# Six PSUM banks of an attention kernel: two each for scores, maxima and the rest, against three by ScalarE and three by VectorE

## The chip, the core and the metric

The kernel runs on one core of a Trainium2 chip. TensorE (PE) multiplies matrices and writes its results into PSUM, which has eight banks here, each holding a tile of 128 partitions x 512 fp32 numbers. ScalarE (ACT) and VectorE (DVE) empty the banks; GpSimd (POOL) works on on-chip memory alone, and SyncE (SP) issues most transfers. The metric is the time of one execution on the device, in microseconds (us). In the profile, PEld is the loading of a weight operand, which runs beside PE.

## What is computed

Attention in which a query sees only the keys of its own hash bucket, then a mixture of eight experts with one expert for each token. Cut to what matters:

```
q_bits = einsum('bhsd,dk->bhsk', q, proj) > 0          # B, H, S, D = 4, 8, 768, 64; 6 bits
k_bits = einsum('bhsd,dk->bhsk', k, proj) > 0
mask   = bucket(q_bits)[..., :, None] == bucket(k_bits)[..., None, :]
scores = where(mask, q @ k.T / sqrt(D), -1e9)
attn   = exp(scores - max); attn = attn / (attn.sum(-1) + 1e-9)
x      = (attn @ v) as 3072 tokens x 512
logits = x @ w_gate + modality_bias[modality_id]; e = argmax(logits); g = softmax(logits)[e]
out    = g * (relu(x @ w1[e]) @ w2[e])                  # 8 experts, 512 -> 1024 -> 512
```

## The kernel before

**Staging.** The 32 heads are worked on as 16 pairs (about 28 us each), then the experts follow. While pair i is scored, the maxima of pair i+1 are taken and pair i+2 is prepared; the weighing of pair i by V lags a few steps. Every four pairs a batch element is finished (`finish`, `finish_x`, `route`).

**The tiles in PSUM.** For each pair there are
- 18 tiles of scores (`score`, L280 and L281, tile `pss`), each emptied by one exponential on ScalarE (L292 or L299). A third of them ("rest") hold 256 columns of both heads;
- 4 pattern products (`patterns`, L207, tile `psx`): the hash bits, multiplied by a pattern, are written beside q and k by two ScalarE operations each (L208, L209);
- 18 tiles of maxima (`maxp`, L224 and L230, tile `psm`), each emptied by one reduction on VectorE (L226 or L232);
- 2 broadcasts of the maxima (`maxp_back`, L249, tile `psx`; "first" with 512 columns and "second" with 256), read by three VectorE operations each (L251 twice, L252);
- one tile each for the bits (L187), the sums of V (L267) and the row sums (L344), in `psx`;
- and what finishing a batch element needs (L359, L367, L385, L403, L598), in `psx`.

Two more banks (`psu`) accumulate the weighing (L326) throughout.

**The banks.** `ps_s` holds two banks for `pss`, `ps_m` two for `psm`, `ps_x` two for everything called `psx`. A pool hands out its banks in turn: a tile takes the bank of the tile two places before it in the same pool, and its first matmul waits until the readers of that older tile are done.

**What sets the order.** PE and SP execute in the order in which the code is written: the strings of `PLAN` (one for each of the six key tiles of a pair) say which generator takes its next step, S a score tile, M a maximum, T or P a step of preparation, B a broadcast, A a step of weighing, V the sums of V, Q the row sums. The last string of a pair ends with `SMTSMTSMBAAB`, the first of the next begins with `LvSPM`: the second and third pattern, the first broadcast, two steps of weighing, the second broadcast, and then the last pattern. ACT, DVE and POOL each execute in an order of their own, which is set when the program is built, from the same code.

**Other lines named later.** L161 copies q or k to a rounded high part `hx` on ScalarE, L163 subtracts it to get the low part (768 columns, both inputs in on-chip memory; on POOL or DVE, and in pairs 9, 10, 13 and 14 on DVE for both halves), L242 spreads the maxima for the broadcast, L302 adds the exponentials into row sums (mostly on POOL, two operations for a key tile).

Of the kernel before, what the change touches and what calls it, by code (L numbers as in the profile page):

```python
# [9 lines left out]
F32 = mybir.dt.float32  # L10
# [6 lines left out]
PSUM = bass.MemoryType.PSUM  # L17

B, H, S, D = 4, 8, 768, 64
NT = S // 128  # L20
HALF = S // 2
MAIN = 512
REST = S - MAIN
NP = B * H // 2
BIG = 2.0 ** 100
CFG = dict(spd=(15,), fxs=3, wy=(0.3, 0.71), hpf=0, he=0, hn=0, hm=0, avp=(1, 2, 3, 4, 5, 6), avs=(2,), early=2, pj=7, w3=(0, 0.9), x3=(0, 1), nmd=1, man=(), man0=2, hpo=0, hpe=0, p0=(0, 1), p1=(0, 0.25), p2=(0, 0.4), p3=(0.4, 0.9), s0=4, rc='DDDD', rq=(1, 2), tq=(3, 3, 1, 1, 0, 0), wh=(0.5, 0.78), ws=(0.78, 1.05), n2=2, psx=2, psm=2, pss=2, npb=5, ut=8, qk=3, v=3, wm=(0, 0.9), wf=(0.04, 1.02), wx=(0.3, 0.71), sub="DPPD", fx='D', fx3='R', raw=4, wp=7, LS=4, LL=7, pn=0, rv=(0,), rs='DDPP', r1=(0, 0.5), r2=(0, 1), avg=1, fub=2, fd=1, pm=(), fj=0, fxe=0.5)
P = 128
# [48 lines left out]


def attention(ctx, actx, tc, a, x_d, route, setup, early_slots, early_tables, latest, adds, bias):
    nc = tc.nc
    v = a["v"]  # L80
# [16 lines left out]
    const = actx.enter_context(tc.tile_pool(name="const", bufs=1))  # L97
    ps_m = actx.enter_context(tc.tile_pool(name="ps_m", bufs=CFG["psm"], space=PSUM))
    ps_s = actx.enter_context(tc.tile_pool(name="ps_s", bufs=CFG["pss"], space=PSUM))
    flags = actx.enter_context(tc.tile_pool(name="flags", bufs=2))  # L100
# [81 lines left out]
    def signs(i):  # L182

        t = st[i]
        z = ps_x.tile([P, MAIN], F32, name="psx")
        for o in range(4):
            nc.tensor.matmul(z[32 * o:32 * o + 32, 0:HALF], zst, t["x"][:, o // 2, (o % 2) * HALF:(o % 2 + 1) * HALF],  # L187
                             start=True, stop=True, tile_position=(0, 32 * o))
        nc.vector.tensor_scalar(out=bits[i % 2], in0=z[:, 0:HALF], scalar1=0.0, scalar2=0.5, op0=ALU.is_gt, op1=ALU.subtract)
        yield  # L190
# [9 lines left out]
    def patterns(i):  # L200

        t = st[i]
        for half in range(2):
            hs = slice(half * HALF, (half + 1) * HALF)
            for h in range(2):
                pp = ps_x.tile([P, MAIN], F32, name="psx")
                nc.tensor.matmul(pp[:, 0:HALF], pat[:, half, h], bits[i % 2], start=True, stop=True)  # L207
                (nc.vector.tensor_copy if i == 0 else nc.scalar.copy)(out=t["m1"][h][PT[h], hs], in_=pp[0:64, 0:HALF])  # L208
                nc.scalar.activation(t["s1"][h][PT[h], hs], pp[64:128, 0:HALF], AF.Relu)  # L209
                if half == 0 and h == 1:  # L210
                    move(t["b"][0][QK[1], 0], t["a"][0][QK[0], 0])
                    move(t["b"][1][QK[0], 1], t["a"][1][QK[1], 1])
                yield

    def maxp(i, late):
# [4 lines left out]
        for qt in range(0, NT, 2):  # L220
            for h in range(2):
                for j in range(2):
                    mp = ps_m.tile([P, MAIN], F32, name="psm")
                    nc.tensor.matmul(mp, t["m1"][h][:, (qt + j) * P:(qt + j + 1) * P], t["s1"][h][:, 0:MAIN], start=True, stop=True)  # L224
                    with tc.high_priority(offset=CFG["hm"]):
                        newest[:] = [nc.vector.tensor_reduce(out=mx[:, qt + j, 1 - h, 0:1], in_=mp, axis=AX.X, op=ALU.max).ins]  # L226
                    yield
                mp = ps_m.tile([P, 2, REST], F32, name="psm")
                for j in range(2):
# [16 lines left out]
    def maxp_back(t, nm, n, cs):  # L246
        bc = ps_x.tile([P, MAIN], F32, name="psx")
        for j in range(n):
# [14 lines left out]
    def vsums(i):  # L263

        a2, vs = st[i]["va"], vsb[i % 2]
        vp = ps_x.tile([P, MAIN], F32, name="psx")
        nc.tensor.matmul(vp[:, 0:P], ones32, a2.rearrange("p h d -> p (h d)"), start=True, stop=True)  # L267
# [69 lines left out]
    def sums(i):  # L337

        b, c = i // 4, i % 4
        if c == 0:  # L340
            gsum[b] = bp.tile([P, HALF], F32, name="gs")
        g = ps_x.tile([P, MAIN], F32, name="psx")
        for j in range(4):
# [7 lines left out]
    def finish(b):  # L351
# [3 lines left out]
        for part in range(2):  # L355
            hs = (slice(0, MAIN), slice(MAIN, S))[part]
            g = ps_x.tile([P, MAIN], F32, name="psx")
            for c in range(4):
# [5 lines left out]
        rv = rin.rearrange("p (a j) (c h) -> p a j c h", a=2, h=2)  # L364
        tp = ps_x.tile([P, 4, P], F32, name="psx")
        for j in range(3):
# [12 lines left out]
        for w in range(2):  # L379
            n = 4 if w == 0 else 2  # L380
            ts = slice(4 * w, 4 * w + n)
            tp = ps_x.tile([P, 4, P], F32, name="psx")
            for j in range(n):
# [6 lines left out]
        yield  # L390
        yield from route(b, lg, ps_x)

    def finish_x(b, lo, hi, pool=bp, n=2, name="xs"):
# [3 lines left out]
        for tt in range(lo, hi):  # L397
            if done:
                done.pop()()
            xs = pool.tile([P, 512], F32, name=name, bufs=n)  # L400
            xp = ps_x.tile([P, 512], F32, name="psx")
            for c in range(4):
# [31 lines left out]
    with tc.manual_schedule(engines={mybir.EngineType.PE, mybir.EngineType.SP}):  # L434
# [17 lines left out]
        avs = weigh()  # L452
# [44 lines left out]
        for _ in avs:  # L497
            pass
        sums(NPR - 1)
    return finish, finish_x, ps_x, ident  # L500


# [518 lines left out]
```

## Time and profile before

| | |
|---|---|
| Median of 3 runs | 800.71 us (800.22 to 800.9) |
| The profiled execution | 798.11 us, of which 796.3 us are its span |
| Granted clock of TensorE over the span | 0.994 |
| Busy share of the span | PE 94%, PEld 66%, DVE 63%, POOL 55%, ACT 52% |

In the page PE reads 9 in nearly every one of the 40 slices. That is not PE at its peak: a matmul of 512 columns is drawn with 0.39 to 0.50 us, but the next one starts 0.23 us after it, so that waits shorter than the overlap disappear from the idle time. Waits are read from the distance of starts.

### The profile page before, as it was taken

To read this page: it belongs to the slowest core of one execution; us is meant where nothing else is said; L and a number is where in the kernel's file an instruction comes from. 1 tells how busy PE (TensorE), PEld (TensorE's weight loads), DVE (VectorE), ACT (ScalarE), POOL (GpSimd) and SP (SyncE) were. 2 spreads that over 40 slices of the span, in tenths; PEclk is the share of its full clock that TensorE was granted. 3 is DMA by queue.
4 is the path that set the end of the run, shared out by engine and by line. 5 is a ranking of instruction groups with operands and counts; after the bars stand their busy time and mean duration, and the time that the engine had idled before them with its cause. 6 is when DMAs were issued, how large, how long until landed. Compare 5 with 4: busy or idle time off the path is not lost.

```text
span 796.3 us, 11626 instructions
## 1 busy us (share of the span) xinstructions
PE 748.0 (94%) x4060; PEld 522.6 (66%) x4060; DVE 505.0 (63%) x839; ACT 413.6 (52%) x730; POOL 438.9 (55%) x321
## 2 busy tenths in 40 slices
PE   4799999999999999997899899999999999999996
PEld 1555556566655566654555555888888888888885
DVE  5777677587787769778769859764244342752422
ACT  3566666666557566664446455324253334633323
POOL 7198988788779978697857694034220204202002
PEclk9999999999999999999999999999999999999999
DMA  6665544254347524465310276466443535833321
GB/s 204 154 179 159 159 119 129 71 159 113 103 123 160 136 83 117 126 153 121 93 48 14 63 161 218 155 90 229 132 159 86 165 101 173 278 134 123 130 54 60
DMA packets 59572, 104.24 MB, mean 131 GB/s; under 512 B 9709, under 2 KB 30829, under 8 KB 59504
## 3 DMA queue, kind: packets, MB, share of 16 engines
q1 hardware_dynamic: 53424, 88.23, 40.0%
q0 software_dynamic: 4928, 13.14, 5.1%
q10 hardware_dynamic: 1152, 2.03, 0.9%
q8 instruction: 34, 0.56, 0.3%
q14 instruction: 34, 0.28, 0.1%
HBM read 59.89 MB, written 13.33 MB: 92 GB/s over the span
## 4 chain that ended last, share of the span: by engine, by line
PE 68%; DVE 11%; issue 10%; ACT 6%; DMA 2%; SPq 1%; POOL 1%; POOLq 0%; ACTq 0%; DVEq 0%
PE psu L326 12%; PE pss L280 8%; PE pss L281 6%; PE hps L812 5%; PE hps L813 5%; PE hps L811 5%; PE yps L857 4%; PE yps L855 4%; PE yps L856 4%; PE psm L224 4%; ACT pb L292 3%; PE psm L230 2%; DVE mx L226 1%; DVE a_0g L251 1%; PE psx L344 1%
## 5 line engine op out<-in xcount | busy, mean ns | idle before, releaser
L302 POOL TENSOR_TENSOR sp<-sp,pb 128x768 f32<-128x768 f32 x124 | 230.9, 1887 | 35.6 <-ACT pb L299 32.2
L292 ACT ACTIVATE pb<-pss 128x512 f32<-128x512 f32 x192 | 113.8, 598 | 104.8 <-PE pss L281 89.4
L226 DVE TENSOR_REDUCE mx<-psm 128x1 f32<-128x512 f32 x192 | 130.7, 687 | 55.2 <-PE psm L224 54.2
L764 DVE TENSOR_TENSOR w<-raw,w 128x1024 fp32r<-128x1024 f32 x64 | 79.5, 1249 | 94.9 <-ACT w L762 66.5
L326 PE MATMUL psu<-pb,vt 128*64 128x512 f32 (+1 forms) x768 | 134.4, 492 | 0.0
L762 ACT CAST w<-raw 128x1024 fp32r<-128x1024 f32 x64 | 66.9, 1050 | 73.8 <-PE yps L857 62.4
L326 PEld LDWEIGHTS psu<-pb,vt 128*64 128x64 f32 x768 | 50.8, 136 | 69.1 <-issue 58.8
L782 POOL DMA_INDIRECT xg<-x_d,tb x18 | 21.9, 1219 | 117.7 <-DMA tb<-tab 113.4
L280 PE MATMUL pss<-a_0g 128*128 128x512 f32 x192 | 80.4, 419 | 3.5 <-ACT pb L292 2.2
L855 PE MATMUL yps<-w,hl 128*128 128x512 f32 x208 | 82.7, 398 | 0.0
L302 POOL TENSOR_TENSOR sp<-pb,pb 128x768 f32<-128x768 f32 x31 | 58.9, 1918 | 41.0 <-ACT pb L299 40.9
L857 PE MATMUL yps<-w,hh 128*128 128x512 f32 x208 | 81.3, 391 | 0.0
L856 PE MATMUL yps<-w,hh 128*128 128x512 f32 x208 | 81.0, 389 | 0.0
L812 PE MATMUL hps<-xl,w 128*128 128x512 f32 x192 | 74.8, 390 | 1.4 <-DVE xl L801 1.4
L811 PE MATMUL hps<-xh,w 128*128 128x512 f32 x192 | 75.5, 393 | 0.0
L813 PE MATMUL hps<-xh,w 128*128 128x512 f32 x192 | 74.8, 390 | 0.0
L232 DVE TENSOR_REDUCE mx<-psm 128x2 f32<-128x512 f32 x96 | 66.1, 689 | 9.6 <-PE psm L230 7.4
L280 PE MATMUL pss<-a_1g 128*128 128x512 f32 x192 | 68.3, 356 | 3.7 <-ACT pb L299 3.4
L817 ACT ACTIVATE hh<-hps 128x512 fp32r<-128x512 f32 x48 | 28.7, 598 | 74.0 <-PE hps L813 71.8
L281 PE MATMUL pss<-b_0g 128*128 128x512 f32 x192 | 65.9, 343 | 0.0
L281 PE MATMUL pss<-b_1g 128*128 128x512 f32 x192 | 65.7, 342 | 0.0
L818 DVE SCALAR_TENSOR_TENSOR hl<-hps,hh 128x512 fp32r<-128x512 f32 x48 | 33.0, 688 | 51.1 <-ACT hh L817 50.5
(203 smaller groups left out, 1374.3 us busy)
## 6 DMA issues: line engine op xcount, KB each, us to landing
raw<-moe_w SPq DMA_DIRECT2D x64, 512.0 KB
xt<-qk SPq DMA_DIRECT2D x31, 384.0 KB
vt<-v SPq DMA_DIRECT2D x16, 384.0 KB
a_0g<-hx SPq DMA_DIRECT2D x30, 192.0 KB
a_1g<-hx SPq DMA_DIRECT2D x30, 192.0 KB
x_d<-xs SPq DMA_DIRECT2D x18, 256.0 KB
b_1g<-a_1g SPq DMA_DIRECT2D x17, 192.0 KB
b_0g<-a_0g SPq DMA_DIRECT2D x17, 192.0 KB
```

The lines of the kernel that those rows point to most:

```text
L226: newest[:] = [nc.vector.tensor_reduce(out=mx[:, qt + j, 1 - h, 0:1], in_=mp, axis=AX.X, op=ALU.max).ins]
L280: nc.tensor.matmul(out, t["s1"][h][:, ks], t["m1"][h][:, cs], start=True, stop=False)
L281: nc.tensor.matmul(out, t["s2"][h][:, ks], t["m2"][h][:, cs], start=False, stop=True)
L292: nc.scalar.activation(t["pb"][kt][:, h, 0:MAIN], sp, AF.Exp, scale=0.125)
L302: add = (nc.vector if h and i in CFG["spd"] else nc.gpsimd).tensor_tensor(out=t["sp"][:, h], in0=(t["pb"][0] if kt == 1 else t["sp"])[:, h ...
L326: nc.tensor.matmul(t["u"][part][64 * h:64 * h + 64, 0:w], t["v"][:, h, kt], t["pb"][kt][:, h, COLS[part]], start=False, stop=(kt == NT - 1 ...
L811: nc.tensor.matmul(hps, lo[:, c, fs], xh[:, c], start=(c == 0), stop=False)
L812: nc.tensor.matmul(hps, hi[:, c, fs], xl[:, c], start=False, stop=False)
L813: nc.tensor.matmul(hps, hi[:, c, fs], xh[:, c], start=False, stop=(c == 3))
L855: nc.tensor.matmul(yps[g], hl[fc][:, gs], hi[:, fb], start=(fc == 0), stop=False)
L856: nc.tensor.matmul(yps[g], hh[fc][:, gs], lo[:, fb], start=False, stop=False)
L857: nc.tensor.matmul(yps[g], hh[fc][:, gs], hi[:, fb], start=False, stop=(fc == 7))
```

## The change

`ps_x`, `ps_m` and `ps_s` hold six banks before and after. After, `ps_s` has three banks for scores and pattern products, all emptied by ScalarE (VectorE does half of it in the first pair). `ps_m` has one bank, and a small class `Banks` hands out the two banks of `ps_x` and this one in turn for all the rest: maxima, broadcasts, bits, sums, finishing. A tile of either kind now takes the bank of the tile three places before it. At the end of attention the one bank is given back, and the two of `ps_x` go on. The two entries `psm` and `pss` of the table of settings are dropped.

```diff
+class Banks:
+
+    def __init__(self, pool, n, last):
+        self.pools = [pool] * n + [last]
+        self.n = 0
+
+    def tile(self, shape, dtype, name):
+        self.n += 1
+        return self.pools[self.n % len(self.pools)].tile(shape, dtype, name="psx")
+
+    def close(self):
+        del self.pools[-1]
...
-    ps_m = actx.enter_context(tc.tile_pool(name="ps_m", bufs=CFG["psm"], space=PSUM))
-    ps_s = actx.enter_context(tc.tile_pool(name="ps_s", bufs=CFG["pss"], space=PSUM))
+    ps_d = Banks(ps_x, CFG["psx"], actx.enter_context(tc.tile_pool(name="ps_m", bufs=1, space=PSUM)))
+    ps_s = actx.enter_context(tc.tile_pool(name="ps_s", bufs=3, space=PSUM))
...
-        z = ps_x.tile([P, MAIN], F32, name="psx")
+        z = ps_d.tile([P, MAIN], F32, name="psx")
...
-                pp = ps_x.tile([P, MAIN], F32, name="psx")
+                pp = ps_s.tile([P, MAIN], F32, name="pss")
...
-                    mp = ps_m.tile([P, MAIN], F32, name="psm")
+                    mp = ps_d.tile([P, MAIN], F32, name="psm")
...
-                mp = ps_m.tile([P, 2, REST], F32, name="psm")
+                mp = ps_d.tile([P, 2, REST], F32, name="psm")
...
-        bc = ps_x.tile([P, MAIN], F32, name="psx")
+        bc = ps_d.tile([P, MAIN], F32, name="psx")
...
-        yield from route(b, lg, ps_x)
+        yield from route(b, lg, ps_d)
...
         sums(NPR - 1)
+        ps_d.close()
     return finish, finish_x, ps_x, ident
```

The other tiles of `ps_x` inside attention (L266, L342, L357, L365, L382, L401) change to `ps_d` in the same way. The lines of the changed kernel are higher by 14 or 15: L207, L224, L249, L251 and L163 are L221, L238, L263, L265 and L177.

On PE and SP every instruction keeps its place. What differs on PE is which tile is in which pool, and what is waited for. Here is PE in the last third of a pair, before, from the second pattern to the maximum before the first broadcast (`pss` scores, `psx_1118` and `psx_1131` patterns, `psm` maxima; numbers are tiles):

```order
L207 MATMUL psx_1118<-bits0_158,pat_157 128x384
L280 MATMUL pss_1124<-a_1g1_114 128x512 [waits Activation_49]
L281 MATMUL pss_1124<-b_1g1_116 128x512
L224 MATMUL psm_1128<-a_1g2_121 128x512 [waits DVE_49]
L207 LDWEIGHTS pat_157
L207 MATMUL psx_1131<-bits0_158,pat_157 128x384
L280 MATMUL pss_1135<-a_0g1_113 128x256 [waits Activation_49]
```

And the same place after:

```order
L221 MATMUL pss_1118<-bits0_158,pat_157 128x384 [waits Activation_49]
L294 MATMUL pss_1124<-a_1g1_114 128x512 [waits Activation_49]
L295 MATMUL pss_1124<-b_1g1_116 128x512
L238 MATMUL psx_1128<-a_1g2_121 128x512 [waits DVE_49]
L221 LDWEIGHTS pat_157
L221 MATMUL pss_1131<-bits0_158,pat_157 128x384 [waits Activation_49]
L294 MATMUL pss_1135<-a_0g1_113 128x256 [waits PE_49,Activation_49]
```

The patterns have moved into the row of the scores: counted three back in it, `pss_1135` takes the bank of the pattern `pss_1118`, and `pss_1124` that of the score tile two scores before it, which it also took before.

On DVE, ACT and POOL the building of the program puts a few instructions in other places. On DVE nearly all of it is L163 (after: L177) of the second half, in the four pairs in which DVE does both halves. Before, between the first broadcast's readers (ending with the `lone` of 512 columns) and the next pair's maxima:

```order
L252 TENSOR_SCALAR lone<-psx 128x512
L251 SCALAR_TENSOR_TENSOR a_0g_113<-psx,a_0g_113 64x256
L251 SCALAR_TENSOR_TENSOR a_1g_114<-psx,a_1g_114 64x256
L252 TENSOR_SCALAR lone<-psx 128x256
L607 TENSOR_REDUCE rsum<-rex 128x6
L226 TENSOR_REDUCE mx<-psm 128x1
...
L232 TENSOR_REDUCE mx<-psm 128x2
L163 TENSOR_TENSOR b_1g_109<-xt,hx 128x768
```

And after:

```order
L266 TENSOR_SCALAR lone<-psx 128x512
L177 TENSOR_TENSOR b_1g_109<-xt,hx 128x768
L265 SCALAR_TENSOR_TENSOR a_0g_113<-psx,a_0g_113 64x256
L265 SCALAR_TENSOR_TENSOR a_1g_114<-psx,a_1g_114 64x256
L266 TENSOR_SCALAR lone<-psx 128x256
L622 TENSOR_REDUCE rsum<-rex 128x6
L240 TENSOR_REDUCE mx<-psx 128x1
```

The subtraction has moved up past 11 to 18 instructions of DVE, to the place between the readers of the two broadcasts. This happens four times in the program. On ACT, nine copies L161 change places with one to three neighbours, on POOL five groups of additions do, and on DVE three maxima come up to three places earlier.

## Rows read from the trace of the kernel before

**Rows 1.** Stage, length; busy PE, PEld, DVE, ACT, POOL; clock, DMA share, GB/s.

```profile
0.00:42.00 42.00, 27.25 (x108) 15.77 (x109) 29.00 (x48) 19.69 (x35) 20.84 (x30) 1.00 0.64 176
42.00:381.00 339.00, 323.33 (x1937) 199.12 (x1937) 256.66 (x438) 215.15 (x415) 282.17 (x190) 0.99 0.48 129
381.00:452.00 71.00, 63.28 (x376) 40.06 (x375) 56.21 (x115) 37.44 (x74) 47.66 (x32) 0.98 0.17 48
452.00:482.00 30.00, 28.36 (x168) 14.92 (x166) 20.08 (x21) 16.52 (x31) 27.71 (x19) 1.00 0.62 141
482.00:796.00 314.00, 305.77 (x1481) 252.69 (x1477) 143.06 (x220) 124.83 (x178) 60.50 (x54) 1.00 0.47 145
```

**Rows 2.** Waits of PE, 42 to 381 us: us in total, times, the longest.

```profile
PE psx L249 <- DMA b_0g<-hx: 3.8, 1, 3.8
PE pss L280 <- ACT pb L299: 2.7, 7, 0.4
PE psx L249 <- ACT nm L242: 2.3, 2, 1.1
PE psm L230 <- DVE mx L226: 1.2, 5, 0.4
PE psx L385 <- DVE lone L252: 1.1, 2, 0.6
PE psx L367 <- DVE lone L252: 1.1, 2, 0.5
PE pss L280 <- ACT pb L292: 0.9, 3, 0.4
```

**Rows 3.** Order of time, end of a pair: start, us, engine, line [idle before, releaser].

```profile
103.15 0.39 PE L224 MATMUL psm<-a_1g 128*128 128x512 f32 x1
103.38 0.34 PE L207 MATMUL psx<-bits,pat 128*128 128x384 bf16 x1
...
104.03 0.50 PE L280 MATMUL pss<-a_1g 128*128 128x512 f32 x1 [0.31 <-ACT pb L299]
...
104.37 0.39 PE L281 MATMUL pss<-b_1g 128*128 128x512 f32 x1
...
104.83 0.49 ACT L209 ACTIVATE a_1g<-psx 64x384 fp32r<-64x384 f32 x1
...
104.88 0.41 PE L280 MATMUL pss<-a_0g 128*128 128x256 f32 x1
```

**Rows 4.** Order of time, beginning of the next pair.

```profile
109.67 0.10 PEld L207 LDWEIGHTS <-pat 128*128 128x128 bf16 x1 [0.37 <-DVE lone L252]
...
111.50 0.30 PEld L230 LDWEIGHTS psm<-a_0g 128*128 128x128 f32 x2 [0.31 <-DVE mx L226]
```

**Rows 5.** All subtractions L163 on DVE: ns minimum/median/maximum, first and last start.

```profile
L163 DVE TENSOR_TENSOR b_1g<-xt,hx x14: 959/1044/2639, 41.6 to 390.4; 128x768 fp32r<-128x768 f32 x14
L163 DVE TENSOR_TENSOR b_0g<-xt,hx x4: 949/2396/5028, 215.5 to 356.5; 128x768 fp32r<-128x768 f32 x4
```

**Rows 6.** Order of time: a slow subtraction, and later a pair's two broadcasts.

```profile
213.49 3.62 POOL L302 TENSOR_TENSOR sp<-sp,pb 128x768 f32<-128x768 f32 x2 [1.77 <-ACT pb L299]
...
215.53 2.40 DVE L163 TENSOR_TENSOR b_0g<-xt,hx 128x768 fp32r<-128x768 f32 x1
...
245.96 3.63 POOL L302 TENSOR_TENSOR sp<-sp,pb 128x768 f32<-128x768 f32 x2
...
247.96 0.43 DVE L251 SCALAR_TENSOR_TENSOR a_0g<-psx,a_0g 64x256 fp32r<-64x256 f32 x1
```

**Rows 7.** Order of time, first maxima of the program.

```profile
19.70 1.29 DVE L226 TENSOR_REDUCE mx<-psm 128x1 f32<-128x512 f32 x2 [0.29 <-PE psm L224]
```

**Rows 8.** Order of time, 15th pair: PE stops for a maximum.

```profile
440.97 0.68 DVE L405 TENSOR_TENSOR xs<-psx,rin 128x512 f32<-128x512 f32 x1
...
443.46 0.50 PE L230 MATMUL psm<-a_1g 128*128 128x256 f32 x2 [2.34 <-DVE mx L226]
```

**Rows 9.** Waits of PE, 452 to 482 us.

```profile
PE pss L280 <- ACT pb L292: 1.2, 5, 0.3
```

More of the change, by code (lines that the diff above doesn't have):

```diff
@@ L25 @@
 BIG = 2.0 ** 100
-CFG = dict(spd=(15,), fxs=3, wy=(0.3, 0.71), hpf=0, he=0, hn=0, hm=0, avp=(1, 2, 3, 4, 5, 6), avs=(2,), early=2, pj=7, w3=(0, 0.9), x3=(0, 1), nmd=1, man=(), man0=2, hpo=0, hpe=0, p0=(0, 1), p1=(0, 0.25), p2=(0, 0.4), p3=(0.4, 0.9), s0=4, rc='DDDD', rq=(1, 2), tq=(3, 3, 1, 1, 0, 0), wh=(0.5, 0.78), ws=(0.78, 1.05), n2=2, psx=2, psm=2, pss=2, npb=5, ut=8, qk=3, v=3, wm=(0, 0.9), wf=(0.04, 1.02), wx=(0.3, 0.71), sub="DPPD", fx='D', fx3='R', raw=4, wp=7, LS=4, LL=7, pn=0, rv=(0,), rs='DDPP', r1=(0, 0.5), r2=(0, 1), avg=1, fub=2, fd=1, pm=(), fj=0, fxe=0.5)
+CFG = dict(spd=(15,), fxs=3, wy=(0.3, 0.71), hpf=0, he=0, hn=0, hm=0, avp=(1, 2, 3, 4, 5, 6), avs=(2,), early=2, pj=7, w3=(0, 0.9), x3=(0, 1), nmd=1, man=(), man0=2, hpo=0, hpe=0, p0=(0, 1), p1=(0, 0.25), p2=(0, 0.4), p3=(0.4, 0.9), s0=4, rc='DDDD', rq=(1, 2), tq=(3, 3, 1, 1, 0, 0), wh=(0.5, 0.78), ws=(0.78, 1.05), n2=2, psx=2, npb=5, ut=8, qk=3, v=3, wm=(0, 0.9), wf=(0.04, 1.02), wx=(0.3, 0.71), sub="DPPD", fx='D', fx3='R', raw=4, wp=7, LS=4, LL=7, pn=0, rv=(0,), rs='DDPP', r1=(0, 0.5), r2=(0, 1), avg=1, fub=2, fd=1, pm=(), fj=0, fxe=0.5)
 P = 128
@@ L265, in vsums @@
         a2, vs = st[i]["va"], vsb[i % 2]
-        vp = ps_x.tile([P, MAIN], F32, name="psx")
+        vp = ps_d.tile([P, MAIN], F32, name="psx")
         nc.tensor.matmul(vp[:, 0:P], ones32, a2.rearrange("p h d -> p (h d)"), start=True, stop=True)
@@ L341, in sums @@
             gsum[b] = bp.tile([P, HALF], F32, name="gs")
-        g = ps_x.tile([P, MAIN], F32, name="psx")
+        g = ps_d.tile([P, MAIN], F32, name="psx")
         for j in range(4):
@@ L356, in finish @@
             hs = (slice(0, MAIN), slice(MAIN, S))[part]
-            g = ps_x.tile([P, MAIN], F32, name="psx")
+            g = ps_d.tile([P, MAIN], F32, name="psx")
             for c in range(4):
@@ L364, in finish @@
         rv = rin.rearrange("p (a j) (c h) -> p a j c h", a=2, h=2)
-        tp = ps_x.tile([P, 4, P], F32, name="psx")
+        tp = ps_d.tile([P, 4, P], F32, name="psx")
         for j in range(3):
@@ L381, in finish @@
             ts = slice(4 * w, 4 * w + n)
-            tp = ps_x.tile([P, 4, P], F32, name="psx")
+            tp = ps_d.tile([P, 4, P], F32, name="psx")
             for j in range(n):
@@ L400, in finish_x @@
             xs = pool.tile([P, 512], F32, name=name, bufs=n)
-            xp = ps_x.tile([P, 512], F32, name="psx")
+            xp = ps_d.tile([P, 512], F32, name="psx")
             for c in range(4):
```

## The prediction

> **What bounds the kernel now.** I read the stages first [rows 1]. The experts (482 to 796 us) keep PE busy for 305.8 of 314 us at the full clock, and the change does not reach them: their transposes go on in the two banks of `ps_x`. So whatever is won or lost lies in attention. There no other engine comes near PE in sum: between 42 and 381 us PE is busy for 323 of 339 us, POOL for 282, DVE for 257, ACT for 215. Then I read the waits of PE [rows 2], to see who ends them. Most waits in this list end when ACT or DVE has emptied a bank (L299, L292, L226, L252); two groups end when the maxima of the first broadcast are ready (L249; the one put down to a DMA is of the same place). Last I read single pairs in order of time [rows 3, 4, 6] to see which tile held the bank, and which tile would hold it when banks are counted three back in the new pools. That count, tile by tile, is the whole argument.
>
> The idle time shown is too small. A 512-column matmul is followed by the next start after 0.23 us (103.15 to 103.38 in [rows 3]). The score at 104.03 shows 0.31 us of idle time, but it starts 0.65 us after the pattern at 103.38, whose 384 columns are worth some 0.17 us at that rate: 0.48 us lost, 0.17 more than shown. And the next start is 0.34 us later, not 0.23 (104.37): its weights could not be loaded ahead. So a shown wait costs about 0.28 us more than its idle time.
>
> **What the change gives, 42 to 381 us.** In [rows 2], the waits of L230 (1.2 us, 5 times), of L385 and L367 (1.1 us, twice each) and of L280 for L292 (0.9 us, 3 times) are for a bank that is two tiles back. Counted three back, each finds a bank that was emptied at least half a microsecond before. The last pattern of a pair waits for the `lone` of a broadcast [rows 4], since both are in `ps_x`; among the scores it finds a bank that has been free for microseconds. The sum is 4.3 us shown in 12 waits, 12 x 0.28 = 3.4 us more, and for waits as the first of [rows 4], which show on PEld alone, I add 1.3: 9 us. The seven waits of L280 for L299 (2.7 us) I leave out. They are of the kind of the one at 104.03, a score between the second and third pattern, and there the third tile back is the same score tile as before: that wait stays.
>
> I take -9, between -11 (a few more short ones) and -4 (half of it comes back at the next wait for the same engine).
>
> **What it takes, in every pair.** With the patterns among the scores there are 22 tiles for ACT on three banks, where 18 had two banks and the patterns had others. The last score before the broadcast starts at 104.88 [rows 3], and then takes the bank of the pattern of 103.38, which ACT lets go of at 104.83 + 0.49 = 105.32. It must wait 0.44 us and the handover, so 0.5. No operation hides it: on PE it stands before the last maximum, the broadcast and the weighing, and all of these start later; ACT itself, which is behind at this point, loses nothing. Between 42 and 381 us I count 11 such places, one in a pair. After three of them PE stops anyhow for the broadcast's maxima (L249: 3.8 once, 2.3 us in two [rows 2]), and arrives in time for that. So 8 x 0.5 = +4, between +2 and +6.
>
> **The subtraction that moves.** In four pairs DVE now does the second L163 ahead of the readers of the second broadcast. Queued behind it: L251 twice, which writes the columns that the third score tile of the next pair reads; L252, which gives the broadcast's bank back; then the next maxima. PE waits for all of them, and its next weighing is some 6 us away. Alone the subtraction takes 0.95 us, but others took 2.40 and 5.03 [rows 5]. The 2.40 one [rows 6] started 0.2 us after the second of two POOL additions (213.49 + 1.81 = 215.30) and ended 0.8 us after that one's end (217.11): it stood still until POOL was done. At 247.96, where one of the four goes, POOL's two additions run until 249.59. There the subtraction would end near 250.4, 2.4 us late; where POOL is nearer its end, 1.5. I take 2.0 for the queue of DVE. PE already loses some 0.5 us at that place (as the second of [rows 4] with its 0.28), so 1.5 x 4 = +6. The bounds are 0 (POOL idle, PE elsewhere late) and 4 x (5.03 - 0.5) = +18. At its old place it stood ahead of the row sums while PE weighed; nobody gets anything back there.
>
> The Trainium skill, SBUF — State Buffer, section Who interferes with whom, states this as a rule: a DVE instruction with two inputs in SBUF and a GpSimd one that reads SBUF share an interface, and whichever issues first holds it for its whole instruction. The 2.40 us row agrees; the 5.03 us row is longer than one addition (half of 3.62 us) and the subtraction together. By the rule no place costs more than 1.81 + 0.95 us, and the term would be at most 4 x (2.76 - 0.5) = +9.
>
> **The other stages.** Up to 42 us DVE takes one maximum after another, and stops 0.29 us for PE every few of them because PE has only two banks ahead [rows 7]; four such stops and a longer one among the first patterns make -1.5 (0 to -2.5). From 381 to 452 us a maximum waits 2.34 us [rows 8] for the maximum two before; three back is the tile that L405 frees at 440.97 + 0.68 = 441.65, so it starts 1.8 us earlier. Two broadcasts' neighbours (L385 and a last pattern) give 1.2 more, and two pairs pay the 0.5 from above: -2 (0 to -4). From 452 to 482 us only scores and weighing are left. Five waits for L292, 1.2 us [rows 9] and 5 x 0.28, are 2.6 us, which the third bank removes; POOL is busy for 27.7 of these 30 us [rows 1] and may keep a part: -2 (0 to -3). The other swaps on ACT and POOL (copies L161 one to three places earlier, additions ahead of sums of V) I cost at 0: what they go past is read a pair or several steps later. If that cover is missing, one costs the 0.8 us of a copy.
>
> **Sum.** -9 + 4 + 6 - 1.5 - 2 - 2 = -4.5 us. Against the profiled execution, 798.11 us (796.3 us of span and 1.8 around it), that is 793.6. The median of the runs is 2.6 us above that execution, so 796.2.
>
> **Rivals.**
> *Given back.* The third bank lets PE run ahead, but the engine that empties the banks has no more time than before; PE then stops one tile later for the same reason. For it: ACT and DVE are behind at exactly these places. Against it: two steps of weighing follow in each pair, in which PE feeds neither, and both catch up (ACT and DVE are busy for two thirds and three quarters of the stage [rows 1]). If a third of the 9 and a third of the 5.5 of the other stages come back (3 and 1.8), the sum is +0.3: no change, 801.0 us. A measurement tells about 0.2%, 1.6 us, from no change. In the Trainium skill, TensorE: Matmul & The Clock Gate, section HAM oscillation — how this bites in real kernels, a kernel is told of in which double-buffering of PSUM gave no further gain; it speaks for this case.
>
> *Scores behind patterns, slower.* The place is the end of each pair. The new wait isn't absorbed by later ones, so 11 x 0.5 = +5.5, while the gain at the pair's start is half, -4, because the maxima there queue behind two broadcasts (2 us of DVE each time) in the one row of three banks. With +6 for the subtraction and -3.5 for the rest that is +4, 804.7 us. It decides from the point where the waits taken away are worth less than 8 us together.
>
> *Subtraction behind POOL, slower.* Each of the four loses against both additions, as in the 5.03 us row: +18 in place of +6, so +7.5, 808 us. For it: one of 18 did. Against it: 14 of the 18 have a median of 1.04 [rows 5].
>
> **Chances.** Forecast 0.55, given back 0.20, scores behind patterns 0.15, behind POOL 0.10. The range takes the forecast's good end (the terms at -11, +3, +5, -2, -3, -2.5: -10.5, 790.2) and goes up past the second rival; it leaves out the third and what lies below: 790 to 805.5. Faster by over 0.2% 0.55, within 0.2% 0.20, slower by over 0.2% 0.25.
>
> **What would show it.** In the changed kernel's waits of PE, L385 and L367 for L252 and L280 for L292 should be gone, and that of the maxima for L226 nearly so; the maximum at 443 should start about 1.8 us sooner against its neighbours. The last score before each broadcast should show a wait for a pattern's second copy (L209's new line) of about half a microsecond. The four moved subtractions should last 1 to 2.5 us, with the third score tile and the next maxima late behind them. Wrong is the forecast if waits of L280 for ACT grow by more than 9 us in sum, or if one of the four lasts 5 us.

## The result, and the profile after

The changed kernel is slower by 1.3%, where faster was forecast, and outside the range.

| | before | after |
|---|---|---|
| Median of 6 runs | 799.73 us | 809.0 us |
| Ratio, 95% interval | | 1.0131 (1.0109 to 1.0153) |
| Span of the profiled execution | 796.3 us | 807.0 us |
| Granted clock over the span | 0.994 | 0.984 |

The answers to [rows 1] and [rows 2] for the changed kernel come first: the stages (columns as there; all stages but the first are some microseconds later now), and the waits of PE between 42 and 381 us (in total, times, the longest).

```profile
0.00:42.00 42.00, 28.14 (x125) 16.44 (x126) 30.94 (x51) 20.95 (x38) 23.64 (x32) 0.96 0.63 171
42.00:381.00 339.00, 314.40 (x1865) 195.09 (x1865) 261.22 (x427) 210.18 (x405) 270.57 (x182) 0.98 0.49 130
```

```profile
PE psx L263 <- ACT nm L256: 11.9, 9, 3.1
PE psx L263 <- DMA b_0g<-hx: 3.5, 1, 3.5
PE pss L294 <- DVE a_0g L265: 3.0, 4, 0.9
PE pss L294 <- ACT a_1g L223: 2.5, 10, 0.3
PE pss L294 <- ACT pb L313: 2.1, 7, 0.3
PE psx L238 <- DVE lone L266: 0.4, 2, 0.2
```

PE gets through 1,865 matmuls in the time of 1,937. The waits that were to go are gone: no L399 or L381 for L266, no L294 for L306, no L244 for L240. In their place L263, the broadcast of the maxima, waits 15.4 us where it waited 6.1. All of these waits are at the second broadcast, the one of 256 columns (two matmuls) behind the two steps of weighing; the prediction and the expectations call it the first broadcast, or its second step.

PE executes the same matmuls in the same order in both kernels, so one can lay the two traces side by side and see at which matmul the changed one falls behind. Grouped by the matmul and the one ahead of it, in us (times of the kernel before; how the small steps are shared between the groups is good to about half a microsecond):

| Place | predicted | measured |
|---|---|---|
| 0 to 42 us: maxima and first patterns, two back | -1.5 | -3.4 |
| 42 to 381: waits for banks two back | -9 | -11.9 |
| 42 to 381: last score for the pattern's bank | +4 | +5.9 |
| 42 to 381: third score tile behind the four moved subtractions | +6 | +4.2 |
| 42 to 381: second broadcast, behind the weighing | 0 | +9.8 |
| 42 to 381: the rest, in small steps | 0 | +3.6 |
| 381 to 452 | -2 | +0.8 |
| 452 to 490 | -2 | +0.3 |
| from 490: experts | 0 | +1.5 |
| Sum | -4.5 | +10.8 |

So the terms of the sum were of the right sign and about the right size in attention's main part. What reversed the result there is a line that the sum didn't have. Its +9.8 are +7.4 in six pairs (1.15 to 1.27 each), +3.6 in one place behind a subtraction of 4.82 us, and -1.2 in three places. The stages behind it add to this: +2.6 where -4 was forecast.

### The profile page after: what moved, and what is told of

Its sections match the earlier page's. It is cut to its first block, busy times and chain, and to the rows that moved or that the text cites. A ratio compares the mean times of both kernels' runs of the same rounds, so it can differ in the third digit from the quotient of the medians.

```text
span 807.0 us, 11676 instructions
## 1 busy us (share of the span) xinstructions
PE 749.4 (93%) x4060; PEld 525.9 (65%) x4060; DVE 518.7 (64%) x839; ACT 413.2 (51%) x730; POOL 437.0 (54%) x321
## 4 chain that ended last, share of the span: by engine, by line
PE 60%; DVE 14%; issue 10%; ACT 7%; POOL 5%; DMA 2%; another core or an unknown queue 1%; POOLq 0%; SPq 0%; ACTq 0%; DVEq 0%
PE psu L340 9%; PE pss L294 7%; PE pss L295 5%; PE hps L826 5%; PE hps L828 5%; PE hps L827 5%; POOL sp L316 4%; PE yps L872 4%; PE yps L870 4%; PE yps L871 4%; PE psx L238 3%; DVE b_1g L177 3%; ACT pb L306 2%; PE psx L244 2%; DVE b_0g L177 2%
## 5 line engine op out<-in xcount | busy, mean ns | idle before, releaser
L316 POOL TENSOR_TENSOR sp<-sp,pb 128x768 f32<-128x768 f32 x124 | 226.6, 1853 | 31.9 <-ACT pb L313 28.8
L306 ACT ACTIVATE pb<-pss 128x512 f32<-128x512 f32 x192 | 114.0, 598 | 100.1 <-PE pss L295 75.6
L240 DVE TENSOR_REDUCE mx<-psx 128x1 f32<-128x512 f32 x192 | 129.4, 685 | 48.2 <-PE psx L238 47.2
L316 POOL TENSOR_TENSOR sp<-pb,pb 128x768 f32<-128x768 f32 x31 | 56.7, 1848 | 51.3 <-ACT pb L313 51.1
L294 PE MATMUL pss<-a_0g 128*128 128x512 f32 x192 | 77.7, 405 | 6.5 <-DVE a_0g L265 3.3
L294 PE MATMUL pss<-a_1g 128*128 128x512 f32 x192 | 68.4, 356 | 2.7 <-ACT pb L313 2.7
L246 DVE TENSOR_REDUCE mx<-psx 128x2 f32<-128x512 f32 x96 | 65.9, 686 | 5.7 <-PE psx L244 4.8
L295 PE MATMUL pss<-b_1g 128*128 128x512 f32 x192 | 66.3, 345 | 0.0
L295 PE MATMUL pss<-b_0g 128*128 128x512 f32 x192 | 66.3, 345 | 0.0
```

The lines of the kernel that those rows point to most:

```text
L294: nc.tensor.matmul(out, t["s1"][h][:, ks], t["m1"][h][:, cs], start=True, stop=False)
L295: nc.tensor.matmul(out, t["s2"][h][:, ks], t["m2"][h][:, cs], start=False, stop=True)
L306: nc.scalar.activation(t["pb"][kt][:, h, 0:MAIN], sp, AF.Exp, scale=0.125)
L316: add = (nc.vector if h and i in CFG["spd"] else nc.gpsimd).tensor_tensor(out=t["sp"][:, h], in0=(t["pb"][0] if kt == 1 else t["sp"])[:, h ...
```

## One pair, before and after

The place of [rows 3], a few more rows of it: POOL's two additions (one row, x2), the ordinary subtraction L163 of the second half, the last reduction of the maxima (L232), what is sent on (L242) and the second broadcast (L249 x2). Columns: start, us, engine, line.

```profile
104.12 4.34 POOL L302 TENSOR_TENSOR sp<-sp,pb 128x768 f32<-128x768 f32 x2 [1.83 <-ACT pb L299]
...
105.36 0.28 PE L281 MATMUL pss<-b_1g 128*128 128x256 f32 x1
...
105.74 1.04 DVE L163 TENSOR_TENSOR b_1g<-xt,hx 128x768 fp32r<-128x768 f32 x1
...
106.71 0.68 DVE L232 TENSOR_REDUCE mx<-psm 128x2 f32<-128x512 f32 x1
...
108.34 0.42 ACT L242 ACTIVATE nm<-m 128x256 fp32r<-128x256 f32 x1 [0.78 <-DVE m L240]
...
108.83 0.36 PE L249 MATMUL psx<-identr,nm 128*128 128x128 f32 x2
```

The same place after:

```profile
97.91 3.61 POOL L316 TENSOR_TENSOR sp<-sp,pb 128x768 f32<-128x768 f32 x2 [0.91 <-ACT pb L313]
...
99.16 0.39 PE L294 MATMUL pss<-a_0g 128*128 128x256 f32 x1 [0.20 <-ACT a_1g L223]
...
99.61 0.28 PE L295 MATMUL pss<-b_1g 128*128 128x256 f32 x1
...
99.99 2.34 DVE L177 TENSOR_TENSOR b_1g<-xt,hx 128x768 fp32r<-128x768 f32 x1 [0.48 <-PE pss L295]
...
102.25 0.68 DVE L246 TENSOR_REDUCE mx<-psx 128x2 f32<-128x512 f32 x1
...
103.88 0.42 ACT L256 ACTIVATE nm<-m 128x256 fp32r<-128x256 f32 x1 [2.54 <-DVE m L254]
...
104.35 0.36 PE L263 MATMUL psx<-identr,nm 128*128 128x128 f32 x2 [1.20 <-ACT nm L256]
```

Before, the subtraction starts 1.62 us after POOL's first addition, which takes some 1.8 us. It takes 0.1 us more than the 0.95 us of an undisturbed one, and POOL's second addition stands still in its turn: the pair of additions lasts 4.34 us instead of 3.61. After, the subtraction starts 2.08 us behind the first addition. Its operand buffer is read by the last score (L295), its start is released by that matmul, and the last score has waited 0.5 us for the pattern's bank. POOL is then 0.3 us into its second addition, the subtraction stands until 101.52, and takes 2.34 us. Behind it on DVE is the last reduction of the maxima, on which the broadcast depends; PE comes out of its 2.8 us of weighing and waits 1.2 us for it. The 0.5 us have become 1.7.

It is so in seven of the ten pairs whose subtractions are shared between DVE and POOL; in the first three (starts at 38.7 to 76.9 us) they last about as long as before. All subtractions of the changed kernel on DVE, for [rows 5]:

```profile
L177 DVE TENSOR_TENSOR b_1g<-xt,hx x14: 1167/2340/2551, 38.7 to 399.0; 128x768 fp32r<-128x768 f32 x14
L177 DVE TENSOR_TENSOR b_0g<-xt,hx x4: 2292/3370/4822, 212.9 to 364.2; 128x768 fp32r<-128x768 f32 x4
```

The seven that took 1.02 to 1.04 us before (at 105.7, 132.1, 160.0, 187.1, 272.1, 299.2 and 390.4) take 2.22 to 2.35. I call this theory **the missed gap**. Its rivals: that the other order on ACT, POOL and DVE slows the subtractions; that the 0.5 us itself, paid in every pair, is the loss; and the four moved subtractions, the prediction's own.

## The experiments

Where lines differ by 14 or 15, the first is that of the kernel before. Times are medians, and ratios are to the kernel before, which ran beside each group at 798.7 to 800.9 us; the changed kernel, 809.0 us, ran beside 799.7.

**1. The last score twice.** In the kernel before:

```diff
-            for h in range(2):
+            for h in (0, 1, 0, 1) if kt == NT - 1 else (0, 1):
                 scores(t, sp[:, h], h, kt, COLS[1])
```

> The kernel before, with the last score tile of each pair (the four matmuls of 256 columns ahead of the last maximum) computed twice into the same bank; nothing else is changed, and the result of the first time is overwritten. It puts what stands behind that tile about 0.47 us later (4 x 0.117), without any wait for a bank. Theory, the missed gap: in the changed kernel this tile waits 0.5 us for a pattern's bank; the ordinary subtraction (L163 of the second half) waits for this tile's last matmul, so it comes 0.5 us later, after POOL has begun the second of its two additions instead of during the first, and stands still until that one ends; the reduction of the last maximum stands behind it on DVE, so the broadcast is late. Then here too the seven subtractions of 1.02 to 1.04 us at the ends of pairs should take 2.2 to 2.4 us, the second step of the first broadcast should wait some 1.2 us more behind the weighing in about nine pairs, and the time is 800 + 16 x 0.47 + 9 x 1.2, about 818 us. Rival, the reordering: the subtractions are slow in the changed kernel because copies, additions and subtractions have other places on ACT, POOL and DVE; then they stay near 1.04 us here and the time is 800 + 7.5, about 807.5 us.

Measured: 826.4 us, ratio 1.0316 (1.0286 to 1.0346). The seven subtractions take 2.33 to 2.35 us, and the broadcast waits as in the changed kernel:

```profile
PE psx L249 <- ACT nm L242: 12.0, 9, 3.4
```

So the kernel before, in its old banks, falls into the same loss when the last score is late. But the expectation held a mistake: the building had also moved the four subtractions of pairs 9, 10, 13 and 14 between the broadcasts, as in the changed kernel. That explains most of the 8 us above the forecast (the third score tile 0.9 to 1.0 us late behind three of them, and one more long subtraction, of 4.71 us with a wait of 3.5), and it means that this run alone doesn't separate delay from order. Runs 7 and 8 do.

**2. The last score ahead of the third pattern**, in the changed kernel:

```diff
-    "SMTSMTSMBAABFGFfFfggehkk",
+    "SMTSMSTMBAABFGFfFfggehkk",
```

> The changed kernel with two letters of the last string of the order exchanged (SMTSMTSM to SMTSMSTM): the last score before the broadcast now stands ahead of the third pattern and takes the bank of a score tile that ScalarE emptied before the second pattern. The building also puts the four moved subtractions back to where they stood in the kernel before. By the missed gap: the 0.5 us wait goes (13 x 0.45 = 6 us), the ordinary subtractions take about 1.0 to 1.3 us again and the second step of the first broadcast no longer waits (about 10 us), the four moved subtractions give back about 3.5: 809 - 19, about 790 us, between 788 and 796. By the reordering: the wait of the last score goes, the subtractions stay at 2.3 us, about 800 us.

Measured: 777.3 us, ratio 0.9701 (0.967 to 0.9732): faster than both kernels, and than expected. Its waits of PE for 41 to 362 us, in full down to 0.2 us, and its subtractions:

```profile
PE pss L294 <- ACT pb L313: 2.1, 7, 0.3
PE pss L294 <- DVE a_0g L265: 0.3, 1, 0.3
PE psx L281 <- DVE rk L626: 0.2, 1, 0.2
```

```profile
L177 DVE TENSOR_TENSOR b_1g<-xt,hx x14: 1128/1164/2565, 41.0 to 371.6; 128x768 fp32r<-128x768 f32 x14
L177 DVE TENSOR_TENSOR b_0g<-xt,hx x4: 948/965/991, 208.5 to 344.3; 128x768 fp32r<-128x768 f32 x4
```

Against the changed kernel, 29.2 us of span: 17.4 at the second broadcast, 6.2 at the last score, 4.2 at the moved subtractions. The first is more than the 10 us expected, since the four first-half subtractions, of which three took 2.40 to 5.03 us even before [rows 5], now take 0.95 to 0.99 too. Three banks by engine are thus worth nearly 3% when the last score doesn't wait.

**3. The four moved subtractions held back**, in the changed kernel:

```diff
-                lo.tensor_tensor(out=b[x][:, x], in0=xs[:, x], in1=hx[:, x].bitcast(F32), op=ALU.subtract)
+                with tc.issue_after(newest[0]) if i in RELIEF and x else nullcontext(): lo.tensor_tensor(out=b[x][:, x], in0=xs[:, x], in1=hx[:, x].bitcast(F32), op=ALU.subtract)
```

> The changed kernel with the four moved subtractions alone held back (second half, pairs 9, 10, 13 and 14): each is queued on VectorE behind the latest maximum or flag in the order of the code, so it runs among the maxima of the next pair and not between the two broadcasts. POOL keeps its order, PE too. If the moved subtraction costs what the trace of the changed kernel shows at these places (third score tile of the next pair 1.0 to 1.1 us late, four times), the time falls by 3.5 to 4.5 us to about 805. If the prediction's 1.5 us or more were right, it falls by 6 or more, 803 or less. If the price only moves to the maxima, 809 stays. The seven ordinary subtractions should stay at 2.2 to 2.4 us, and the waits of the first broadcast's second step too.

Measured: 802.3 us (10 runs, 798.3 to 809.5), ratio 1.003 (0.9998 to 1.0061). It gave 6.7 us, not 4. At the four places the trace gives back 4.2 us, as forecast; another 3.2 us are one wait of 3.5 us behind a first-half subtraction of 4.4 us at 364 us, which here took 0.96 us. The broadcast still waits 12.1 us in nine places. The runs of this kernel spread over 11 us, so the parts are read from the trace. So the moved subtractions are a part of the loss, and the smaller one.

**4. Patterns back among the maxima**, scores alone on three banks:

```diff
-                pp = ps_s.tile([P, MAIN], F32, name="pss")
+                pp = ps_d.tile([P, MAIN], F32, name="psx")
```

> The changed kernel with the pattern products back among the maxima: three banks for scores alone, three for maxima, patterns and all else. The last score then takes the bank of the score three scores back, long emptied; the wait of the score between second and third pattern (0.25 to 0.7 us in each pair, in both kernels) should go too. By the missed gap: subtractions of about 1.0 to 1.6 us, no wait at the first broadcast's second step (-10), no wait of the last score (-6), and some of -5 at the score between the patterns; patterns may now wait for maxima (+0 to +6): about 792 us, 787 to 799. By the reordering: 2.3 us subtractions stay and the time is about 800 to 803. Two of the four moved subtractions stay where the changed kernel has them, two go back.

Measured: 792.3 us, ratio 0.9909 (0.988 to 0.9937), in the middle of what the missed gap gave. The seven subtractions take 1.10 to 1.60 us. New are waits of the maxima, some of them behind patterns, which ACT empties (last two rows):

```profile
PE psx L238 <- DVE rsum L622: 3.5, 2, 1.8
PE psx L238 <- DVE lone L266: 2.8, 4, 1.4
PE psx L244 <- ACT a_1g L223: 2.4, 8, 0.3
PE psx L238 <- PE psx L221: 2.2, 3, 0.7
```

**5. The exchange of run 2 in the kernel before**, banks as they were.

> The kernel before, with its banks as they were, and the same two letters exchanged as in the run e2_swap (the last score ahead of the third pattern). Theory, both are needed: before, the patterns have banks of their own and the last score waits for none of them, so the exchange takes no wait away; the subtraction's trigger comes some 0.17 us earlier and stays inside POOL's first addition (1.0 to 1.3 us each). The waits for banks two back stay. About 800 us, 797 to 802. Rival, the order alone did it: the exchange itself is what made e2_swap fast, and the time is 777 to 785 us.

Measured: 802.5 us, ratio 1.002 (0.9996 to 1.0045): no change. The exchange is worth nothing without the banks, and the banks lose without the exchange.

**6. Every subtraction of DVE held back**, in the changed kernel (the edit of run 3 with `i > 1 and lo is nc.vector`):

> The changed kernel with every subtraction of VectorE (from the second prepared pair on) queued behind the latest maximum or flag in the order of the code: it leaves the place between the last two reductions ahead of the broadcast. The last score still waits 0.5 us for the pattern's bank. By the missed gap: the waits of the broadcast's second step go (9 x 1.27 = 11 us, and 3.6 of the one long one), the four moved ones give what e3_relief_late gave (7 us); the 0.5 us waits stay. What the subtractions do among the maxima is new: up to 2.3 us each on VectorE, with three banks of lead on PE: 0 to 1 us each. 809 - 20 + 0 to 14: about 793 us, 788 to 802. Rival, the 0.5 us of the last score is the main cost and the subtraction only shows it: then the broadcast's step keeps its wait and the time stays at 802.

Measured: 791.9 us, ratio 0.9899 (0.9855 to 0.9942), as expected. The last score still waits (second row, as in the changed kernel), no broadcast does, and 17 us are gone. Half of what the broadcast gives back stood behind the seven subtractions, the other half behind the four first-half ones, which this edit holds back too:

```profile
PE psx L244 <- DVE mx L240: 5.1, 2, 3.1
PE pss L294 <- ACT a_1g L223: 2.6, 11, 0.3
```

This parts the wait from what stands behind it: the 0.5 us stay and the loss goes. The first row is new: two maxima behind late subtractions of 3.93 and 2.90 us.

**7 and 8. One matmul more, or two.** In the kernel before, as run 1 but shorter: one matmul of 256 columns ahead of the last score (`e9_quarter`),

```diff
-            sp = ps_s.tile([P, 2, REST], F32, name="pss")
+            sp = ps_s.tile([P, 2, REST], F32, name="pss"); kt == NT - 1 and nc.tensor.matmul(sp[:, 0], t["s1"][0][:, kt * P:(kt + 1) * P], t["m1"][0][:, COLS[1]], start=True, stop=True)
```

or two (`e10_half`: run 1's edit with `(0, 0, 1)`).

> The kernel before with one more matmul of 256 columns (0.117 us) ahead of the last score tile of each pair, overwritten by what follows. In the kernel before the ordinary subtraction starts 0.20 to 0.23 us before the end of POOL's first addition and runs between the two; 0.12 us later it should still be in time: the seven stay near 1.0 us and the first broadcast's second step does not wait in these pairs. The building also puts the four subtractions of pairs 9, 10, 13 and 14 between the broadcasts, as in the changed kernel (3.5 to 7 us). 800 + 16 x 0.12 + 3.5 to 7: 805 to 809 us. If every delay of the last score were paid in proportion to its length (the rival), about a quarter of the 26 us of e1_last_twice, the same 806, but then e10_half gives 813.

> As e9_quarter, with two matmuls more in place of one (0.234 us); the orders of VectorE, ScalarE, POOL and SyncE are the same as in e9_quarter, instruction for instruction. The subtraction now starts when POOL has begun its second addition, or with it: by the missed gap the seven take 2.3 to 2.6 us and the second step of the first broadcast waits 1.3 to 1.6 us in these pairs (7 x 1.4 = 10 us), so the whole price falls between one matmul and two: e9_quarter + 16 x 0.12 + 10, some 818 to 823 us. By a price in proportion to the delay: e9_quarter + 4 to 7, 810 to 815, with subtractions between 1.0 and 2.3 us.

Measured: 806.5 us, ratio 1.0128 (1.0102 to 1.0154), and 824.9 us, ratio 1.0316 (1.0272 to 1.036). The same pair in the first and in the second, POOL's additions and DVE's subtraction and reduction:

```profile
104.44 4.40 POOL L302 TENSOR_TENSOR sp<-sp,pb 128x768 f32<-128x768 f32 x2 [1.80 <-ACT pb L299]
...
106.19 0.96 DVE L163 TENSOR_TENSOR b_1g<-xt,hx 128x768 fp32r<-128x768 f32 x1
...
107.07 0.69 DVE L232 TENSOR_REDUCE mx<-psm 128x2 f32<-128x512 f32 x1
```

```profile
104.05 3.63 POOL L302 TENSOR_TENSOR sp<-sp,pb 128x768 f32<-128x768 f32 x2 [1.81 <-ACT pb L299]
...
105.91 2.59 DVE L163 TENSOR_TENSOR b_1g<-xt,hx 128x768 fp32r<-128x768 f32 x1 [0.25 <-ACT pb L292]
...
108.42 0.68 DVE L232 TENSOR_REDUCE mx<-psm 128x2 f32<-128x512 f32 x1
```

1.75 us behind the first addition the subtraction is in time (0.96 us), 1.86 us behind it is not (2.59). The orders on DVE, ACT, POOL and SP are the same in both kernels, and 16 times 0.117 us on PE make 18 us. (Some 3.7 of them are one more subtraction of 5.0 us, a first-half one, at 379 us.) By a price in proportion to the delay it would have been 4 to 7. These two runs show the missed gap, and exclude the reordering as the cause of the seven slow subtractions.

**9. One of POOL's additions left out**, in the changed kernel:

```diff
-                for h in range(2):
+                for h in range(1 if kt == 4 and i < NPR - 1 else 2):
```

> The changed kernel without the second of POOL's two additions for the fifth key tile of pairs 0 to 14 (the row sums of one head lack that tile): the addition that the late subtraction is thought to stand behind. Nothing on PE depends on it in time. By the missed gap: the subtractions at the ends of the pairs take about 1.0 us although the last score still waits 0.5 us and the order on VectorE is the changed kernel's; the waits of the broadcast's second step go (about 11 us), and the subtraction of 4.8 us, which stands behind two additions, falls as well (3.6 us): about 795 us, 792 to 799. If something else slows the subtractions (transfers, ScalarE's writes), they stay at 2.2 to 2.4 us and the time at 807 or more.

Measured: 800.0 us, ratio 1.0 (0.9986 to 1.0014), and the seven subtractions still take 2.38 to 2.40 us: a miss. In the trace POOL's own subtraction (L177 of the first half) has moved up into the place of the addition and starts 0.25 us ahead of DVE's. What I took away was replaced by work of the same length, so the run tells little on the seven. The one long subtraction does answer. It took 4.82 us behind two additions; the rows are DVE's and POOL's of the changed kernel, then those of this run with one addition (the first row of each is an indirect transfer that POOL issues):

```profile
242.42 0.95 POOL L634 DMA_INDIRECT tab<-recs,posi  x1 [0.30 <-issue]
...
242.99 4.82 DVE L177 TENSOR_TENSOR b_0g<-xt,hx 128x768 fp32r<-128x768 f32 x1 [0.34 <-DMA b_1g<-a_1g]
...
243.40 3.58 POOL L316 TENSOR_TENSOR sp<-sp,pb 128x768 f32<-128x768 f32 x2
```

```profile
241.95 0.96 POOL L634 DMA_INDIRECT tab<-recs,posi  x1 [0.30 <-issue]
...
242.56 3.02 DVE L177 TENSOR_TENSOR b_0g<-xt,hx 128x768 fp32r<-128x768 f32 x1 [0.34 <-DMA b_1g<-a_1g]
...
242.94 1.82 POOL L316 TENSOR_TENSOR sp<-sp,pb 128x768 f32<-128x768 f32 x1
```

It is shorter by 1.80 us, one addition: POOL is what this subtraction stands behind. Three of the four moved ones, with less of POOL in their way, take 0.94 us. The 9 us against the changed kernel come mostly from the four first-half subtractions (6.9 us at the broadcasts behind them; three now take 0.96 us), the rest from the moved ones and from POOL's earlier end ahead of the experts.

**10. Runs 2 and 6 together**:

> e2_swap with every subtraction queued behind the latest maximum or flag, as in e6_all_late. In e2_swap the subtractions take 1.13 to 1.17 us in most pairs and nothing waits at the broadcast, so by the missed gap there is little left to win there: 774 to 778 us. If among the maxima they meet two additions of POOL, 0.5 us or more is lost in each of 14 pairs, and it is slower, 782 or more.

Measured: 786.9 us, ratio 0.9824 (0.9807 to 0.9841), 10 us slower than run 2. With the exchange the subtractions have a good place ahead of the broadcast; among the maxima two first-half ones of 3.30 us cost PE 4.9 us, as in run 6, and the weighing behind these two stops, at a granted clock of 0.75 (245 to 250 us) and 0.66 (360 to 365 us), 3.6 more. I expected no loss as the likelier. The time fell into the second case, but not in its way: most of the other subtractions take 0.95 us and cost nothing.

**11. Runs 2 and 4 together**:

> e4_scores_alone with the two letters exchanged as in e2_swap: scores alone on three banks, patterns among the maxima, the last score ahead of the third pattern. What e2_swap still loses at the score between the patterns (eight waits of 0.3 us shown, some 4 us) would go; but the patterns, which ScalarE empties, stand in the row that VectorE empties, where e4_scores_alone shows waits of the maxima behind patterns (L244 for L223 2.4 us, L238 behind L221 2.2 us and others of about 6). If the partition by the engine that empties a bank matters, this is slower than e2_swap: 783 to 792 us. If only the last score's wait mattered, 772 to 778 us.

Measured: 787.5 us, ratio 0.9857 (0.9829 to 0.9886), as the partition by engine gave. Scores on banks of their own lose 10 us to scores with patterns, since the maxima then stand behind ACT: the trace gives some 6 us back at the score between the patterns and takes about 12 at maxima that stand behind patterns.

## Why the prediction was wrong, step by step

- **Waits for banks two back** (-9, to -11): right in mechanism, a little small at -11.9. Not half of it came back at the next wait for the same engine, but a part did: in six pairs in which a batch element is finished, eight starts, most of them of maxima, are 0.28 to 0.39 us late, since the bank three back in VectorE's row is now the one that comes late. That is +2.5 of the +3.6 in small steps, so the term is worth some -9.4. The first 42 us gave -3.4 instead of -1.5, and the maximum at 443 us started 1.64 us sooner against its neighbours, as read (1.8).
- **The last score's wait** (+4): its length was right, 0.5 to 0.6 us in eleven places (+5.9). That three of them would be absorbed by the broadcast's waits was right in one place and half right in two: these waits are shorter by 0.68, 0.25 and 0.24 us. The failing step is the sentence on what the wait delays: PE's own work, ACT "loses nothing". DVE was not asked. The subtraction was taken as an operation of fixed length that stands elsewhere, yet it is released by exactly this tile, and the last reduction of the maxima stands behind it. That is +7.4 us in the main stage, and 1.3 in the next one, where the sum had nothing.
- **The evidence was in the rows.** The prediction read the 2.40 us case of [rows 6] and priced POOL's additions at four moved places. Against that price being general it set "14 of the 18 have a median of 1.04" [rows 5]. That median wasn't a property of the subtraction but of the phase: in the rows above, seven of the 18 start 0.2 us before POOL would have started its next addition. A delay of 0.5 us had to be held against that margin.
- **The moved subtractions** (+6, 0 to +18): +4.2, about 1 us each; they lasted 1.52 to 2.55 us, where 1 to 2.5 was said. Where the prediction put its upper end (two additions, as in the 5.03 us row), a first-half subtraction that isn't moved took 4.82 us and cost 3.6 us. Such a subtraction stands before the change too (5.03 us, at 356.5 us); in the changed kernel there are two (4.82 and 4.38), and the sum had no term for it.
- **381 to 452 us and after** (-4): the relieved waits came (L294 for L306 is gone, -3.3 us by 475 us), but the moved and slow subtractions go on to 399 us, and PE waits 2.8 us for POOL's last additions ahead of the row sums at 490 us. Between 381 and 452 us two relieved waits came back almost whole. The pattern at 398 us starts 1.44 us sooner against its neighbours, and the second maximum behind it 1.67 us later; the maximum at 443 us starts 1.64 us sooner, and one 7 us later is 1.32 us late. Both wait for VectorE, in the row of three banks (in the second place VectorE itself stands 1.6 us for a transfer); the rows are of the changed kernel:

```profile
408.16 0.47 PE L238 MATMUL psx<-a_0g 128*128 128x512 f32 x1 [1.71 <-DVE gl L400]
...
459.69 0.50 PE L238 MATMUL psx<-a_1g 128*128 128x512 f32 x1 [1.17 <-DVE mx L246]
```

The sum is +1.1 to 490 us, and 1.5 more in the experts, which is not explained.
- **The rivals.** Given back happened in part: 2.5 us in the main stage and 3.0 in the next, 5.5 in sum where this rival had 4.8. By this rival's own sum (+0.3) that alone leaves no change. Scores behind patterns named the right wait, with no more than its own length, at 804.7. Subtraction behind POOL came within a microsecond, at 808, by the wrong instances: four moved ones at 4.5 us each, where it was mostly the unmoved ones at 1.2 us each: near in time by luck. None of them had what stands behind the wait.

The chances followed from this: the slower cases were given 0.25, because a term of +8.7 was nowhere to be bounded. What is not settled: why a single addition's end suffices for some subtractions, while those of 4.4 us and more stand through two additions. Where it happens, the thirteen traces do show: of their 234 subtractions on DVE, 17 were passed by an operation that POOL began later, and in all 17 POOL's additions follow directly on one of its indirect transfers (L634 or L619, as in the rows of run 9). No other subtraction was passed.

## What to carry to other kernels

A wait is to be priced by what it releases on the other engines, not by its length: list each instruction that the waiting one lets go, and look how much margin that one has against its neighbours. VectorE and GpSimd mostly took turns by whole instructions here, so that 0.1 us decided over 1.6 us in every turn of a loop; a median near the undisturbed time tells nothing of that margin. And banks by the engine that empties them are worth 3% here, once the order on PE is chosen such that no tile stands right behind a slow one in its new row.

## What the hardware showed that was not expected

The margin is sharp. In run 7 the subtraction is issued 0.05 to 0.07 us ahead of POOL's next addition and takes 0.96 us; in run 8 it is issued 0.06 to 0.07 us behind it, and takes 2.57 to 2.59. All seven in each run agree within 0.02 us. The Trainium skill, SBUF — State Buffer, section Who interferes with whom, says this: whoever issues first holds the shared interface for its whole instruction. These runs agree with it. The 17 that were passed do not: at 242.99 us above DVE is 0.41 us ahead of POOL's first addition, and still lasts until both are over.

TensorE's clock fell behind stops of PE. In the changed kernel PE finished its weighing at 246.3 us and had nothing to do until 249.83. The stretches of 5 us there, granted clock third from the right:

```profile
240.00:245.00 5.00, 4.50 (x27) 2.58 (x27) 3.81 (x4) 4.35 (x9) 4.50 (x4) 1.00 0.89 149
245.00:250.00 5.00, 1.46 (x11) 0.46 (x6) 4.91 (x6) 0.42 (x1) 4.81 (x4) 0.84 1.14 246
250.00:255.00 5.00, 4.64 (x15) 3.23 (x16) 4.94 (x8) 2.04 (x4) 3.80 (x3) 0.50 0.73 211
```

0.50 is the lower of the two levels, 1.2 GHz. In stretches of 5 us up to 500 us the changed kernel shows the lower level five times (within 20 to 30, 245 to 260, 370 to 380, 405 to 415 and 490 to 495 us), each time behind a stop of PE of 1.8 to 3.5 us. The kernel before shows it twice: 0.75 from 365 to 370 us, after its stop of 3.8 us at 363 us, and 0.82 and 0.84 from 395 to 405 us, where PE was busy for 3.1 and 3.6 of 5 us. From these stretches the lower level lasts 24 us against 7, which by an estimate from them costs 8.5 us at most; the starts show less, since PE stood still for a part of it. Behind the stop at 246 us they come some 1.4 us later in sum, which is in the small steps of the table. The fall to 0.66 from 490 to 495 us, after the wait for the row sums, made 16 transposes last 3.17 us instead of 1.97, but these 1.2 us did not reach the end: the kernel before waits 1.4 us for an operand behind them (L812), and the changed one does not.
